# First chunk of a fused attention and expert kernel: last rows loaded in three portions, weight words asked for five blocks ahead, squares of the values behind the attention

## Chip, cores and metric

The kernel runs on one core of a Trainium2 chip. The metric is the device time of one execution in microseconds (us), as the median over runs. Engines are named as in the profile: PE (TensorE matmul, PEld its weight loads), DVE (VectorE), ACT (ScalarE), POOL (GpSimd) and SP (SyncE, which issues nearly all transfers here). PEclk is the clock granted to PE: 1.00 is 2.4 GHz, 0.50 is 1.2 GHz.

## What is computed

The reference is causal attention with a linear memory, mixed by a gate per head, then a dense squared-ReLU layer, then four experts mixed by normalised weights:

```python
scores = scale * np.matmul(q, k.transpose(0, 1, 3, 2))      # causal mask, softmax over keys
local = np.matmul(a, v)
mem_out = einsum(phi(q), M_prev) / (einsum(phi(q), z_prev) + 1e-06)
attn = g * mem_out + (1 - g) * local                          # g = sigmoid(beta)
h = np.maximum(x @ w_in, 0.0); y = (h * h) @ w_out            # x: attention, 1152 x 512; d_ff 2048
p = domain_probs / (domain_probs.sum(-1, keepdims=True) + 1e-09)
out += p[:, e:e + 1] * (np.maximum(y @ w1[e], 0.0) @ w2[e])   # four experts, d_ff 1024
```

Sizes: 2 sequences, 8 heads, 576 rows, head width 64. The dense layer's weights arrive as 64-bit words and are turned into 32-bit floats on the chip.

## The kernel before

The 1152 rows are cut into nine tiles of 128 rows (`TILES`) and three chunks of tiles (`CHUNKS`): chunk 0 is the first 128 rows of both sequences, chunk 1 is four tiles (rows 128 to 383), chunk 2 is the rest. The dense layer runs over 16 blocks of 128 hidden units, once per chunk, by `ffn1(c, ...)`. Its first run, `ffn1(0)`, is the stage this change touches; it starts near 22 us and ends near 136 us. Three streams of work run in it side by side:

- **The layer.** For each block f, `up(f)` multiplies the chunk by the up-weights (matmuls of L101, output `hpa`), ACT and DVE square the ReLU (L744, L745), and `down(f - 2)` multiplies by the down-weights (L759, outputs `y`). One step of the layer is one matmul of the program (two MATMUL records of the trace).
- **The weights.** `convert` takes 32 halves of blocks ("words", tile `w64`, 512 KB each, L682). ACT makes two pieces from a word (L694 `mag`, L697 `bits`), DVE joins them (L700, L703) and SP writes the result to DRAM (L706, `w1s`) for the two later runs. `fetch(i + 3)` asks for the word three places on. Words alternate between the tags `w0` and `w1` of pool `wp`, two buffers each, so four words have room. In this text words are counted from 0; word 9 is `w_529` in the built program before and `w_471` in the changed one.
- **The attention of chunk 1.** `attention_a` works in pairs of units over 12 pairs. `rest` sorts the parts of each pair into a list of steps: scores (L302) two pairs ahead, row maxima by `top` on DVE (L189), exponentials on ACT (L319), transposes of the probabilities on PE (L331) copied by ACT (L336), and products with the values (L351). The last steps combine memory and local parts (L213 on DVE, L214 on POOL and DVE), transpose each tile (`second`, L197, output `tp`, one PSUM buffer of tag `m`) and split it into two floats (L222 on ACT, L223 on DVE), which is what the next layer run (L106) reads.

`mix(layer, rest(...), 0.58)` takes 0.58 steps of `rest` per step of the layer, so the two are interleaved on PE in a fixed order: PE runs in program order, and what it must wait for, it waits for in place. The order on ACT, DVE, POOL and SP is chosen by the framework's scheduler when the program is built, except where `keep_in_program_order` pins an instruction; on the chip each of them runs its list in order.

Two more parts matter here. `load(r)` asks for the keys, queries and values of row block r (L271, L272, L280); `load(2)` is planned as one step at the end of pair 0. `value_scale` squares all values on ACT (L439, ten instructions: six on value tiles `va`, four on tiles `vstage` that it loads itself, L430, two buffers), adds the sums with a matmul (L443, output `total`, also PSUM tag `m`), and makes from it a power of two, `vs` (L444 and `power`), which chunk 2's attention reads later (L528). In `rest`, `value_scale` advances after steps 0 and 3 of each pair from the third on:

```python
for k, (_, f) in enumerate(sorted(at_i[i], key=lambda x: x[0])):
    f()
    if k in (0, 3) and i > 1:
        next(scale, None)
    yield
```

Of the kernel before, what the change touches and what calls it, by code (L numbers as in the profile page):

```python
# [10 lines left out]
F32 = mybir.dt.float32  # L11
# [3 lines left out]
I32 = mybir.dt.int32  # L15
# [6 lines left out]
P = 128  # L22
B, H, S, D = 2, 8, 576, 64
DM = 512
# [28 lines left out]
def attention_then_experts(ctx, tc, qa, ka, va, qc, kc, vc, mz, beta, w1, probs, w2, out):  # L53
# [11 lines left out]
    nc = tc.nc  # L65
# [7 lines left out]
    wp = ctx.enter_context(tc.tile_pool(name="wp", bufs=2))  # L73
# [39 lines left out]
    def run(g):  # L113
        for _ in g:
            pass
# [111 lines left out]
    ka_t, va_t = {}, {}  # L227
# [29 lines left out]
    def attention_a(c, pool, eng, banks):  # L257
# [6 lines left out]
            pairs += [[(t + b, kn, h, nh) for b in range(B)] for h in range(0, H, nh)]  # L264
        st, q, a_, at_, pvs, xls = {}, {}, {}, {}, {}, {}

        def load(r):
            raw = pool.tile([P, H, P], F32, tag="qa", name="qa", bufs=2)
            ka_t[r] = kva.tile([P, H, P], F32, name=f"ka{r}")
            for hs in (slice(0, 4), slice(4, 8)):  # L270
                nc.sync.dma_start(out=ka_t[r][:, hs], in_=ka[r, :, hs])  # L271
                nc.sync.dma_start(out=raw[:, hs], in_=qa[r, :, hs])  # L272
            q[r] = [raw, None, pool.tile([P, B, H, D + 1], F32, tag="xm", name="xm", bufs=2)]
            if r:
                load_v(r)

        def load_v(r):
            for b in range(B):
                va_t[b, r] = kva.tile([P, H, D], F32, name=f"va{b}_{r}")
                nc.sync.dma_start(out=va_t[b, r].rearrange("p h d -> p (h d)"), in_=va[b, r])  # L280
# [132 lines left out]
        def out_(b):  # L413
# [3 lines left out]

        return SimpleNamespace(
            pairs=pairs, load=load, load_v=load_v, phis=phis, scores=s_, turn=t_, values=v_, mem=mem, combine=combine_,
            states=states, norms=norms, recall=recall, weights=weights, local=local, out=out_,  # L420
        )
# [27 lines left out]
    def rest(x, scale):  # L449

        at_i = {}

        def plan(i, order, f):
            at_i.setdefault(i, []).append((order, f))

        plan(0, 5, lambda: x.load(2))
        for i, pair in enumerate(x.pairs):
            t, kn, h0, nh = pair[0]
            r = TILES[t][0][1] // P
            if i:  # L460
                plan(i - 2, 0, lambda p=pair: run(x.scores(p)))
            for u in pair:
                plan(i, 2, lambda u=u: x.turn(u))
            plan(i, 4, lambda p=pair: [x.values(u) for u in p])
            if h0 == 0:
                plan(i - (r > 1), 1, lambda r=r: [run(y) for y in x.phis(r)])
                for g, hs in enumerate((slice(0, 3), slice(3, 6), slice(6, 8))):
                    plan(i + g // (3 - r), 3, lambda r=r, hs=hs: x.mem(r, hs))
            if h0 + nh == H:
                for n, u in enumerate(pair):  # L470
                    parts = []

                    def make(t=u[0], parts=parts):
                        parts.extend(x.combine(t))
                        parts[0]()

                    plan(i, 5 + n, make)
                    plan(i, 7 + n, lambda parts=parts: parts[1]())
                    plan(i + 1, 1.5 + n, lambda parts=parts: parts[2]()())
        for i in sorted(at_i):  # L480
            for k, (_, f) in enumerate(sorted(at_i[i], key=lambda x: x[0])):
                f()
                if k in (0, 3) and i > 1:
                    next(scale, None)
                yield

    def attention_b(pool, ps):

# [184 lines left out]
    def convert(pool):  # L673

        todo = [x for g in range(n1 + 2) for x in ((g, 0), (g - 2, 1)) if 0 <= x[0] < n1]
        words = {}

        def fetch(i):
            if i < len(todo):
                f, half = todo[i]  # L680
                words[i] = wp.tile([P, DM, 2], I32, tag=f"w{i % 2}", name="w64")
                nc.sync.dma_start(out=words[i].rearrange("p n t -> p (n t)"), in_=w1[f, half].bitcast(I32))  # L682

        fetch(0)
        yield
        fetch(1)
        fetch(2)
        yield
        for i, (f, half) in enumerate(todo):
            fetch(i + 3)  # L690
            w64 = words.pop(i)
            mag = pool.tile([P, DM], F32, tag="mag", name="mag")

            nc.scalar.activation(out=mag, in_=w64[:, :, 1].bitcast(F32), func=AF.Abs, scale=2.0**-112)  # L694
            bits = pool.tile([P, DM], I32, tag="bits", name="bits", bufs=8)

            nc.scalar.activation(out=bits, in_=w64.bitcast(U8)[:, :, 3], func=AF.Copy, scale=2.0**-5, bias=-31.0 / 64)  # L697
            if i == 0:
                yield
            nc.vector.scalar_tensor_tensor(  # L700
                out=bits, in0=mag.bitcast(I32), scalar=3, in1=bits, op0=ALU.logical_shift_left, op1=ALU.bitwise_or
            )
            nc.vector.scalar_tensor_tensor(  # L703
                out=bits, in0=w64[:, :, 1], scalar=-(2**31), in1=bits, op0=ALU.bitwise_and, op1=ALU.bitwise_or
            )
            nc.sync.dma_start(out=w1s[f, half], in_=bits.bitcast(F32))  # L706
            made[f, half] = bits.bitcast(F32)
            yield
# [77 lines left out]
    with ExitStack() as ca:  # L786
        kva = ca.enter_context(tc.tile_pool(name="kva", bufs=1))
        aap = ca.enter_context(tc.tile_pool(name="aap", bufs=2))
        cvp = ca.enter_context(tc.tile_pool(name="cvp", bufs=2))
        cv = convert(cvp)  # L790
        mzd = kva.tile([P, H, B, D + 1], F32, name="mzd")
        with tc.tile_pool(name="ps_0", bufs=1, space=PSUM) as ps_0:
# [21 lines left out]
        with tc.tile_pool(name="ps_1", bufs=1, space=PSUM) as ps_1:  # L814
            banks[:] = ps_1, 2, 1, 1
            layer.send(ps_1)
            mix(layer, rest(c1, value_scale(aap, banks)), 0.58)
# [262 lines left out]
    for i in range(len(pairs)):  # L1080
# [5 lines left out]
        todo = iter([(j, half) for j in {0: (), 1: (4, 5), 2: (6, 7)}.get(i, (i + 5,)) for half in range(2)])  # L1086
# [80 lines left out]
```

## Time and profile before

| what | us |
|---|---|
| median of three runs (lowest, highest) | 718.51 (717.93, 721.85) |
| the profiled execution, its own time | 718.66 |
| its span, first to last instruction | 716.8 |
| around the span (718.66 - 716.8) | 1.9 |
| PE busy in the span | 676.4 (94%) |
| DVE busy | 553.3 (77%) |
| ACT busy | 428.0 (60%) |
| mean granted PE clock | 0.994 |

Busy PE time is a modelled figure of pipelined matmuls, so it shows where PE stood idle better than how close it is to its peak. Idle time of another engine costs nothing unless PE, or a transfer that PE needs, waits for it. Over the whole span DMA is busy about half the time; in the first quarter it is close to full in places.

### The profile page before, as it was taken

How to read it: one execution, taken by the hardware profiler on the slowest of the kernel's cores; microseconds unless marked ns; L12 is line 12 of the kernel's file. 1: busy time of each engine (PE TensorE's matmuls, PEld its weight loads, DVE VectorE, ACT ScalarE, POOL GpSimd, SP SyncE). 2: the span in 40 equal slices, each digit the busy share in tenths (PEclk: the TensorE clock that was granted, in tenths of full speed). 3: DMA queues.
4: the chain of work that ended last, by engine and by line, in shares of the span. 5: the costliest groups of instructions: out<-in, count | busy, mean ns of one | idle time of the engine just before them, and what ended most of it. 6: DMA issues, size and time to landing. Idle time of an engine off the chain costs nothing.

```text
span 716.8 us, 12523 instructions
## 1 busy us (share of the span) xinstructions
PE 676.4 (94%) x4604; PEld 480.9 (67%) x4604; DVE 553.3 (77%) x1107; ACT 428.0 (60%) x842; POOL 168.9 (24%) x198
## 2 busy tenths in 40 slices
PE   7788899999899998999999999999999999999997
PEld 5567677877678787999765565666655555555553
DVE  6878866499998865778798778998786776867763
ACT  5879786586565546986876648455453444444340
POOL 1001101232010032102243332544323232232300
PEclk9999999999999999999999999999999999999999
DMA  9996883378976544875313231333333131100002
GB/s 314 321 323 232 268 279 115 129 245 212 209 177 133 126 103 125 304 269 149 117 61 112 66 118 59 119 117 118 118 123 114 59 118 59 59 1 1 1 1 73
DMA packets 65421, 101.25 MB, mean 141 GB/s; under 512 B 32656, under 2 KB 34704, under 8 KB 65360
## 3 DMA queue, kind: packets, MB, share of 16 engines
q1 hardware_dynamic: 65216, 100.45, 45.5%
q8 instruction: 36, 0.59, 0.3%
q14 instruction: 25, 0.20, 0.1%
q10 hardware_dynamic: 144, 0.00, 0.0%
HBM read 82.87 MB, written 10.75 MB: 131 GB/s over the span
## 4 chain that ended last, share of the span: by engine, by line
PE 36%; DVE 8%; DMA 3%; ACT 2%; issue 2%; POOL 1%; DVEq 0%; ACTq 0%; SPq 0%; POOLq 0%
PE o L1055 19%; PE pe L963 16%; DMA raw<-in_w 3%; DVE wu L927 2%; DVE w L872 1%; DVE g L979 1%; DVE h L984 1%; ACT junk L868 1%; DVE xs L872 1%; ACT g L978 1%; ACT wu L932 0%; DVE acc L1068 0%; DVE u L984 0%; POOL u L993 0%; DVE w L84 0%
## 5 line engine op out<-in xcount | busy, mean ns | idle before, releaser
L1055 PE MATMUL o<-w,g 128*128 128x512 f16 x864 | 218.3, 379 | 7.1 <-DVE g L979 3.6
L963 PE MATMUL pe<-xs,wu 128*128 128x256 f16 (+1 forms) x1344 | 196.4, 286 | 1.6 <-DVE h L984 1.6
L963 PEld LDWEIGHTS <-wu 128*128 128x128 f16 x1344 | 130.9, 98 | 69.7 <-issue 3.4
L1055 PEld LDWEIGHTS <-g 128*128 128x128 f16 x864 | 83.8, 98 | 77.4 <-DVE g L979 6.6
L978 ACT ACTIVATE g<-h 128x512 f16<-128x512 f32 (+1 forms) x64 | 43.3, 677 | 105.7 <-DVE h L984 105.7
L761 PE MATMUL y<-g,w 128*128 128x512 f32 (+1 forms) x384 | 89.4, 369 | 0.0
L761 PEld LDWEIGHTS y<-g,w 128*128 128x128 f32 x384 | 67.7, 188 | 7.2
L979 DVE SCALAR_TENSOR_TENSOR g<-h,g 128x512 f16<-128x512 f32 (+1 forms) x64 | 50.5, 789 | 25.7 <-ACT g L978 25.5
L993 POOL TENSOR_TENSOR u<-u,p 128x256 f32<-128x256 f32 (+1 forms) x32 | 32.4, 1014 | 132.1 <-ACT p L992 111.3
L930 POOL TENSOR_TENSOR ws<-raw 128x256 f32<-128x256 f32 x32 | 23.3, 728 | 159.6 <-issue 79.7
L84 DVE TENSOR_TENSOR w<-wraw,w 128x512 fp32r<-128x512 f32 x64 | 47.8, 753 | 14.0 <-ACT w L83 13.9
L984 DVE SCALAR_TENSOR_TENSOR h<-pe,u 128x256 f32<-128x256 f32 (+1 forms) x96 | 42.9, 452 | 19.8 <-PE pe L963 15.6
L106 PE MATMUL hpb<-x,w 128*128 128x512 f32 x192 | 51.0, 401 | 4.2 <-DVE r L745 4.2
L927 DVE SCALAR_TENSOR_TENSOR wu<-ws,wpow,wu 128x512 f16<-128x512 f32 x64 | 50.0, 823 | 1.0 <-ACT wu L938 0.9
L872 DVE SCALAR_TENSOR_TENSOR w<-raw,wpow,w 128x512 f16<-128x512 f32 x64 | 48.2, 757 | 0.7 <-ACT w L871 0.6
L83 ACT ACTIVATE w<-wraw 128x512 fp32r<-128x512 f32 x64 | 39.6, 624 | 14.8 <-DMA wraw<-w1s 7.4
L868 ACT ACTIVATE junk<-raw 128x1024 bf16<-128x1024 f32 x32 | 33.6, 1050 | 20.0 <-DMA raw<-in_w 19.8
L871 ACT ACTIVATE w<-raw,wpow 128x512 f16<-128x512 f32 x64 | 44.6, 709 | 0.9 <-PE o L1055 0.9
L106 PEld LDWEIGHTS hpb<-x,w 128*128 128x128 f32 x192 | 34.9, 188 | 12.6 <-DVE r L745 5.9
L189 DVE CUSTOM_DVE_ANT_0 a<-sc,mask 128x384 f32<-128x384 f32 (+4 forms) x80 | 35.8, 479 | 7.3 <-PE sc L551 7.0
L210 POOL TENSOR_TENSOR xm<-xm,cf 128x512 f32<-128x512 f32 x7 | 8.1, 1162 | 138.0 <-DVE cf L209 94.7
L106 PE MATMUL hpc<-x,w 128*128 128x384 f32 x192 | 37.0, 338 | 1.4 <-DVE w L84 0.5
(168 smaller groups left out, 1153.2 us busy)
## 6 DMA issues: line engine op xcount, KB each, us to landing
raw<-in_w SPq DMA_DIRECT2D x64, 512.0 KB, 3.4
w<-in_w SPq DMA_DIRECT2D x32, 512.0 KB, 5.2
wraw<-w1s SPq DMA_DIRECT2D x64, 256.0 KB, 3.1
w1s<-bits SPq DMA_DIRECT2D x32, 256.0 KB, 3.3
kraw<-in_kc SPq DMA_DIRECT2D x8, 576.0 KB, 3.9
vraw<-in_vc SPq DMA_DIRECT2D x8, 320.0 KB, 4.0
qraw<-in_qc SPq DMA_DIRECT2D x4, 512.0 KB, 4.2
out<-acc SPq DMA_DIRECT2D x8, 256.0 KB, 2.1
```

What stands on the lines that cost most here:

```text
L84: eng.tensor_sub(w[:, 1], raw, w[:, 0].bitcast(F32))
L106: nc.tensor.matmul(acc, lhsT=w[:, a, kk * P:(kk + 1) * P], rhs=xs_r[c][:, b, kk, :], start=(i == 0), stop=(i == 3 * NK - 1),)
L761: nc.tensor.matmul(yacc[d], lhsT=w[:, a, d * P:(d + 1) * P], rhs=g[:, b], start=(first and i == 0), stop=(last and i == 2),)
L868: nc.scalar.activation(out=junk2, in_=raws[i, half], func=AF.Square, accum_out=wsq[:, e, half, p:p + 1])
L871: nc.scalar.activation(out=w0, in_=x, func=AF.Copy, scale=s)
L872: nc.vector.scalar_tensor_tensor(out=w1, in0=x, scalar=s, in1=w0, op0=ALU.mult, op1=ALU.subtract)
L927: nc.vector.scalar_tensor_tensor(out=w[:, 1, ks], in0=x, scalar=s1, in1=w[:, 0, ks], op0=ALU.mult, op1=ALU.subtract)
L963: nc.tensor.matmul(acc, lhsT=w[:, wa, k, kk * P:kk * P + P], rhs=x[:, xb, kk], start=(m == 0), stop=(m == 5))
L978: nc.scalar.activation(out=g[:, 0], in_=hm, func=AF.Relu)
L979: nc.vector.scalar_tensor_tensor(out=g[:, 1], in0=hm, scalar=0.0, in1=g[:, 0], op0=ALU.max, op1=ALU.subtract)
L984: nc.vector.scalar_tensor_tensor(out=out, in0=acc, scalar=HID, in1=x, op0=ALU.mult, op1=ALU.add)
L1055: nc.tensor.matmul(outs[t], lhsT=g[:, gb, r:r + P], rhs=w[:, wa], start=(p == 0 and m == 1 and k == 0), stop=(p == 3 and m == 0 and k == 2),)
```

## The change

`load` takes portions: 0 and 1 are the two halves (by heads) of keys and queries, 2 the values. `rest` plans the three portions of `load(2)` as steps of pairs 0, 1 and 2 (first half, values, second half) where one step stood at the end of pair 0; the list of steps is two longer. `value_scale` advances after every step from pair 10 on, and what is left of it runs at the end. Words go to three tags of two buffers each, the third from `convert`'s own pool, and from the second word on `fetch` is called for the words three, four and five places on, each word once.

```diff
-        def load(r):
...
+        def load(r, parts=(0, 1, 2)):
+            if 0 in parts:
+                ka_t[r] = kva.tile([P, H, P], F32, name=f"ka{r}")
...
+            for i in parts:
+                hs = slice(4 * i, 4 * i + 4)
+                if i < 2:
+                    nc.sync.dma_start(out=ka_t[r][:, hs], in_=ka[r, :, hs])
+                    nc.sync.dma_start(out=q[r][0][:, hs], in_=qa[r, :, hs])
+                elif r:
+                    load_v(r)
...
-        plan(0, 5, lambda: x.load(2))
+        for i, k, order in ((0, 0, 5), (1, 2, 5), (2, 1, 5)):
+            plan(i, order, lambda k=k: x.load(2, (k,)))
...
                 f()
-                if k in (0, 3) and i > 1:
+                if i > 9:
                     next(scale, None)
                 yield
+        yield from scale
...
-        words = {}
+        words, fetched = {}, set()
 
         def fetch(i):
-            if i < len(todo):
+            if i < len(todo) and i not in words and i not in fetched:
                 f, half = todo[i]
-                words[i] = wp.tile([P, DM, 2], I32, tag=f"w{i % 2}", name="w64")
+                fetched.add(i)
+                words[i] = (pool if i % 3 == 2 else wp).tile([P, DM, 2], I32, tag=f"w{i % 3}", name="w64")
...
-            fetch(i + 3)
+            for k in range(3 if i else 1):
+                fetch(i + 3 + k)
```

Line numbers of the changed program are some 3 to 7 higher than before from `load` on. Three places show how it moves instructions.

On SP, at the start of the layer, before: each write of a converted word (L706) is followed by one request for a word (L682), with two loads of `vstage` and three of `wraw` (weights for the next layer run) among them.

```order
L706 DMA w1s<-bits 128x512
L682 DMA w_398<-in_w 128x1024
L430 DMA vstage<-in_vc 128x4x128
L706 DMA w1s<-bits 128x512
L682 DMA w_419<-in_w 128x1024
L430 DMA vstage<-in_vc 128x4x128
L706 DMA w1s<-bits 128x512
L682 DMA w_458<-in_w 128x1024
L706 DMA w1s<-bits 128x512
L682 DMA w_467<-in_w 128x1024
L706 DMA w1s<-bits 128x512
L682 DMA w_520<-in_w 128x1024
```

The same place in the changed program (L713 is the write, L688 the request):

```order
L713 DMA w1s<-bits 128x512
L688 DMA w_398<-in_w 128x1024
L688 DMA w_400<-in_w 128x1024
L688 DMA w_402<-in_w 128x1024
L713 DMA w1s<-bits 128x512
L688 DMA w_423<-in_w 128x1024
L713 DMA w1s<-bits 128x512
L688 DMA w_462<-in_w 128x1024
L713 DMA w1s<-bits 128x512
L688 DMA w_471<-in_w 128x1024
L713 DMA w1s<-bits 128x512
L688 DMA w_524<-in_w 128x1024
```

Words 4, 5 and 6 now follow the first write, and word 9 (`w_471`) the fourth, where before word 9 (`w_529`) followed the sixth write; the three `wraw` loads have gone to a place behind some twenty more writes.

On DVE, before the row maxima (L189) of the fourth pair of chunk 1, before:

```order
L700 SCALAR_TENSOR_TENSOR bits<-mag,bits 128x512
L703 SCALAR_TENSOR_TENSOR bits<-w_520,bits 128x512
L700 SCALAR_TENSOR_TENSOR bits<-mag,bits 128x512
L189 ISA a,mx<-sc,mask 128x256
L189 ISA mx 128x1
```

And changed:

```order
L707 SCALAR_TENSOR_TENSOR bits<-mag,bits 128x512
L710 SCALAR_TENSOR_TENSOR bits<-w_462,bits 128x512
L707 SCALAR_TENSOR_TENSOR bits<-mag,bits 128x512 x2
L710 SCALAR_TENSOR_TENSOR bits<-w_471,bits 128x512
L189 ISA a,mx<-sc,mask 128x256
L189 ISA mx 128x1
```

Ahead of the maxima now stand two joins more, those of words 9 and 10.

On PE at the end of the stage, behind the last product with the values, before:

```order
L759 MATMUL y_417<-g_1343,bits 128x256 x2
L759 MATMUL y_418<-g_1343,bits 128x256 x2
L101 MATMUL hpa<-y_77,bits 128x256 x4
L759 MATMUL y_417<-g_1419,bits 128x256
L197 MATMUL tp<-ident,xl 128x128 x4
L759 MATMUL y_417<-g_1419,bits 128x256
L759 MATMUL y_418<-g_1419,bits 128x256
L197 MATMUL tp<-ident,xl 128x128 x4
```

Changed, on PE and then on ACT (L442 is the square, L222 the split of a transposed tile):

```order
L101 MATMUL hpa<-y_77,bits 128x256 x4
L766 MATMUL y_421<-g_1361,bits 128x256 x2
L766 MATMUL y_422<-g_1361,bits 128x256 x2
L197 MATMUL tp<-ident,xl 128x128 x4
L446 MATMUL total<-vsq,ones 128x10
L766 MATMUL y_421<-g_1440,bits 128x256 x2
L197 MATMUL tp<-ident,xl 128x128 x4
L766 MATMUL y_422<-g_1440,bits 128x256 x2
```

```order
L361 ACTIVATE xl<-pv 128x2x256
L442 ACTIVATE sq,vsq<-va_2_705 128x512
L442 ACTIVATE sq,vsq<-vstage 128x512 x2
L751 ACTIVATE g_1504<-hpa 128x256
L222 ACTIVATE x_75<-tp 128x4x128
L442 ACTIVATE sq,vsq<-vstage 128x512 x2
L222 ACTIVATE x_75<-tp 128x4x128
```

The matmul of `total` has moved from the middle of the stage to a place between the two transposes, directly behind the first, and the squares that it sums stand on ACT among the last copies of the stage. No instruction order differs on any engine behind this stage.

## Rows read from the trace of the kernel before

**Rows 1.** Windows: busy us (and instructions) of PE, PEld, DVE, ACT, POOL, then PEclk, DMA share, GB/s.

```profile
60.00:80.00 20.00, 18.05 (x160) 14.66 (x158) 16.24 (x34) 17.19 (x43) 3.09 (x2) 1.00 0.74 238
...
120.00:140.00 20.00, 19.45 (x136) 16.21 (x135) 7.45 (x12) 8.29 (x24) 1.49 (x1) 1.00 0.28 92
sum 120.00, PE 106.68 PEld 84.61 DVE 84.61 ACT 90.59 POOL 9.54; mean PE 17.78 PEld 14.10 DVE 14.10 ACT 15.10 POOL 1.59
```

**Rows 2.** Timeline of PE: start us, us, what, count, idle before and its releaser.

```profile
46.94 1.09 PE L331 MATMUL atp<-ident,a 128*128 128x128 f32 x4 [2.55 <-DVE mx L189]
47.82 1.92 PE L759 MATMUL y<-g,bits 128*128 128x256 f32 x4
...
50.04 1.03 PE L759 MATMUL y<-g,bits 128*128 128x256 f32 x4
...
57.07 0.66 PE L331 MATMUL atp<-ident,a 128*128 128x128 f32 x4 [1.05 <-DVE mx L189]
...
67.74 1.17 PE L351 MATMUL pv<-va,at 128*64 128x64 f32 x32 [0.76 <-ACT at L336]
```

**Rows 3.** Timeline of ACT around the wait for a word.

```profile
40.55 0.66 ACT L697 ACTIVATE bits<-w 128x512 int32<-128x512 uint8 x1
44.18 0.66 ACT L694 ACTIVATE mag<-w 128x512 f32<-128x512 f32 x1 [2.97 <-DMA w<-in_w]
```

**Rows 4.** Timeline of DVE at the same place.

```profile
45.42 0.69 DVE L700 SCALAR_TENSOR_TENSOR bits<-mag,bits 128x512 int32<-128x512 int32 x1 [2.74 <-ACT bits L697]
46.03 0.42 DVE L189 CUSTOM_DVE_ANT_0 a<-sc,mask 128x256 f32<-128x256 f32 x1
```

**Rows 5.** Timeline of SP: the first write, requests of words 7 to 9, loads of `wraw`.

```profile
22.50 0.33 SPq L706 DMA_DIRECT2D w1s<-bits  x1
...
31.03 0.38 SPq L682 DMA_DIRECT2D w<-in_w  x1
...
33.55 0.45 SPq L682 DMA_DIRECT2D w<-in_w  x1
34.05 1.42 SPq L723 DMA_DIRECT2D wraw<-w1s  x3
...
38.94 0.38 SPq L682 DMA_DIRECT2D w<-in_w  x1
```

**Rows 6.** Windows around that wait, columns as in rows 1.

```profile
42.00:44.00 2.00, 2.00 (x21) 1.51 (x20) 0.68 (x1) 0.00 (x0) 0.00 (x0) 1.00 0.80 253
...
47.00:48.00 1.00, 1.00 (x5) 1.00 (x6) 1.00 (x8) 1.00 (x4) 0.00 (x0) 0.50 1.03 412
```

**Rows 7.** Timeline of PE, later: the middle of the stage and its end.

```profile
76.80 0.55 PE L331 MATMUL atp<-ident,a 128*128 128x128 f32 x3 [1.01 <-DVE mx L189]
...
81.86 0.94 PE L364 MATMUL pm<-mzd,phia 128*128 128x130 f32 x6 [1.59 <-DVE x L223]
...
125.53 1.99 PE L759 MATMUL y<-g,bits 128*128 128x256 f32 x8
...
129.52 0.60 PE L197 MATMUL tp<-ident,xl 128*128 128x128 f32 x4
...
131.54 0.66 PE L197 MATMUL tp<-ident,xl 128*128 128x128 f32 x4 [0.55 <-DVE x L223]
```

**Rows 8.** Timeline of ACT: a square with its accumulator read, and copies of the end.

```profile
79.89 0.62 ACT L439 ACTIVATE sq<-va 128x512 bf16<-128x512 f32 x1
80.40 0.19 ACT L439 ACTIVATION_READ_ACCUMULATOR sq<-va 128x1 f32 x1
80.50 0.58 ACT L222 ACTIVATE x<-tp 128x512 fp32r<-128x512 f32 x1
...
125.65 0.60 ACT L358 ACTIVATE xl<-pv 128x512 f32<-128x512 f32 x1 [0.47 <-PE pv L351]
...
130.16 0.60 ACT L222 ACTIVATE x<-tp 128x512 fp32r<-128x512 f32 x1 [0.48 <-PE tp L197]
```

**Rows 9.** Tile `vstage`: the time from issue to landing of its four loads.

```profile
DMA to landing us min/median/max: 3.5/5.0/5.4
```

More of the change, by code (lines that the diff above doesn't have):

```diff
@@ L265, in attention_a @@
         st, q, a_, at_, pvs, xls = {}, {}, {}, {}, {}, {}
-        def load(r):
[L268 to L275, printed above, removed]
+        def load(r, parts=(0, 1, 2)):
+            if 0 in parts:
+                ka_t[r] = kva.tile([P, H, P], F32, name=f"ka{r}")
+                q[r] = [pool.tile([P, H, P], F32, tag="qa", name="qa", bufs=2), None, None]
+                q[r][2] = pool.tile([P, B, H, D + 1], F32, tag="xm", name="xm", bufs=2)
+            for i in parts:
[5 more added lines that the diff above has]
+                    load_v(r)
         def load_v(r):
```

## The prediction, made blind

> **What bounds the kernel now.** I read the windows first, to see where PE stands idle near the change. From 20 to 140 us PE is busy 106.68 of 120 us [rows 1], so 13.3 us is all that any new order in this stage can give back, apart from the clock. ACT is busy 17.19 us of the 20 between 60 and 80, and 8.29 us of the last 20 [rows 1]: the squares leave a full stretch for an emptier one.
>
> The timeline of PE then gives the single waits. The longest one in which the change has a part ends at 46.94: 2.55 us, named after DVE's maxima [rows 2]. Followed back, it is not DVE that is slow. ACT stood idle 2.97 us until 44.18 for a word [rows 3], the join of that word on DVE waited 2.74 us for ACT, and the maxima stand behind this join in DVE's list [rows 4]. The word was asked for only at 38.94, behind a gap in SP's list that words 7 and 8 (31.03, 33.55) did not have [rows 5]; it took 44.18 - 38.94 = 5.2 us. The engines of the DMA were not full meanwhile (share 0.80) [rows 6], so the request was late, not the transfer slow. The wait has a second price: behind it the granted clock is 0.50, the level of 1.2 GHz [rows 6]. Four transposes take 1.09 us and four layer matmuls 1.92 there, against 0.66 and 1.03 at 2.4 GHz [rows 2]: 0.43 + 0.89 = 1.3 us lost.
>
> **The change part by part.** The first three parts give, the last one takes.
>
> *Load in portions.* In SP's list all six loads still stand ahead of the first write, only in another order (values before second halves). I count it as nothing: what covers it is that no engine reads these tiles before the third pair. The two more steps in the list shift attention by 2 / 0.58 = 3.4 layer steps against the layer; PE's work stays.
>
> *Words five ahead.* Word 9 is now asked for behind the fourth write, where word 7 was (31.03), word 10 where word 8 was (33.55) [rows 5]. Are they there when ACT is free, at 40.55 + 0.66 = 41.2 [rows 3]? From the first write at 22.5 on, words 4 to 10 (seven times 524 KB) and five writes (262 KB each) make 5.0 MB: 12.1 us at 412 GB/s, 19.7 us at 253 [rows 6], so all of it is there between 34.6 and 42.2. ACT takes two pieces of 0.6 us from each word: word 9 until 42.4, word 10 until 43.6. DVE must now join both before the maxima, 0.61 us apiece (45.42 to 46.03 [rows 4]): start of word 10 by 44.2, rest of word 9 by 44.9. PE went 0.91 us after the maxima began (46.94 - 46.03), so now at 45.8; it gets there at 44.4 and waits 1.4 us in place of 2.55. **Gain 1.15 us**, and as no such long wait is left, **1.3 us** of clock. Bounds: 0, where the words come no sooner, and 2.55 + 1.3 = 3.9.
>
> *Less ahead of the waiting engines.* The wait of 1.05 us at 57.07 and that of 1.01 at 76.80 are again for the maxima [rows 2, 7]. In the changed list of DVE one pair of joins fewer (1.2 us) stands ahead of each: I take 0.9 and 0.7. Before the 0.76 us at 67.74 [rows 2] a square sat on ACT between the exponentials and the copies that PE waits for; a square costs 0.61 (79.89 to 80.50 [rows 8]), so 0.6 goes. At 81.86 [rows 7] a square sat ahead of the copy of `tp`; a piece of a word takes its place, but one layer step more covers it: 0.4 of 1.59. Together **2.6 us**; bounds 0 and 4.4, the four waits whole.
>
> *Squares at the end.* Let T be the end of the last product with values, 125.53. A layer step takes (129.52 - 125.53) / 9 = 0.44 us [rows 7]. Behind T now stand eight steps and the first transposes, so PE comes to the matmul of `total` at T + 3.55 + 0.5 = T + 4.0. It needs all ten squares. ACT copies the product from T + 0.1 (125.65 [rows 8], 0.5 us), then does squares 5, 6 and 7 until T + 2.45. The loads for squares 8 and 9 need the two buffers which 6 and 7 read, so SP can ask for them at T + 1.85 and T + 2.45 and not before. Such a load took 3.5, 5.0 or 5.4 us [rows 9], the long ones in the full stretch; here the DMA share is 0.28 [rows 1], so I take 3.5: T + 5.4 and T + 6.0. Square 9 ends at T + 6.6, its accumulator read 0.1 later (rows of 0.62 and 0.19, overlapped [rows 8]): T + 6.7. **PE waits 2.7 us.** Below, with loads that land at once, the copy of `tp` comes 0.64 us after the transposes begin and takes 0.6 [rows 8], T + 4.8, then two squares: T + 6.1, a wait of 2.1. Above, with 5.4: T + 8.6, a wait of 4.6. The old wait of 0.55 us at 131.54 [rows 7] goes, since two layer steps stand between `total` and the second transposes: net **2.15** (1.55 to 4.05). The nearest row for the clock behind such a wait is that of 2.55 us, behind which it fell, so I add the same **1.3** (0 to 1.3). The sum and the eight small DVE instructions for `vs` lie under two layer steps and the second transposes; even at the 0.42 us of a maximum [rows 4] each, 3.4 in all, the second copy is split by T + 11, when the stage ends. Three loads of `wraw` and two of `vstage` leave the early stretch; they have the 0.28 of the end.
>
> Sum: -1.15 - 1.3 - 2.6 + 2.15 + 1.3 = -1.6. Nothing behind the stage moves in any list, so it arrives whole: 718.66 - 1.6 = 717.06 on the profiled execution's time. The median is 0.15 below that execution (718.51), so **716.9 us**. About 0.5%, 3.6 us, is what a measurement of this kernel can tell from no change.
>
> **The rivals.**
>
> 1. *The last loads land fast.* If `vstage` lands in under 2.9 us, PE waits 2.1 to 2.3 us; say that the clock then stays at 2.4 GHz, as it does from 60 to 80 us with waits up to 1.01 in it [rows 1, 7]: 718.66 - 5.05 + 1.65 = 715.3, by the median 715.1. For it: the quiet DMA. Against: no load of this shape under 3.5 [rows 9]. The Trainium skill, in "DMA: Bandwidth & Descriptors", section on the anatomy of one DMA, fits transfers issued by GpSimd with about 2.0 us plus the bytes over 436 GB/s; for 256 KB that makes an estimate of 2.6 us, and this rival. The trace's shortest, 3.5, speaks against it, but in busier stretches.
>
> 2. *Slower: DVE's joins become the wait.* With more words on hand, joins run in front of the maxima at many pairs, as at the second place shown, where two more stand. If this takes back what the shorter lists gave (2.6) and the wait at 46.94 still costs the clock, only 1.15 is gained: 718.66 - 1.15 + 3.45 = 720.96, median 720.8. It decides if PE's waits for the maxima between 50 and 120 us stay at 2 us or more in total. For it: DVE is busy 84.61 of 120 us [rows 1] and runs its list in order. Against: the stage's joins are the same number, and words come sooner.
>
> 3. *The transfers are the bound.* If the early words share the same full engines, word 9 comes no sooner and 2.45 goes from the gain: 719.5, median 719.4. For it: at 253 GB/s the bytes end at 42.2. Against: 412 GB/s in the same stretch [rows 6].
>
> 4. *The last loads land late*, 5.4 us: 718.66 - 5.05 + 4.05 + 1.3 = 718.96, median 718.8.
>
> That a part doesn't do what it says is in the sum already: the portions change next to nothing.
>
> **How the numbers follow.** Chances: forecast 0.47, rival 1 0.22, rival 2 0.11, rival 3 0.08, rival 4 0.12. The range goes from 713.5 (rival 1 with 1.6 us more of the four waits' 4.4) to 720.9 (rival 2). It leaves out a wider gain and a stacking of rivals 2 and 4. Faster by over 0.5% means under 714.9: half of rival 1 and the forecast with most of its bounds on the good side, 0.2. Slower means over 722.1, which only rivals 2 and 4 together reach: 0.07. The rest, 0.73, is no change that can be told.
>
> **What would show it.** Right: ACT's wait for a word near 41 us gone; PE's idle before the transposes there 1.4 us or less, and clock 1.00 behind it; a wait of PE at `total` of 2 to 3 us, ended by the last square, with a lower granted clock behind. Wrong: `total` without a wait over 1 us, the early wait still there, or PE's busy share between 50 and 120 us no higher than before.

## The result and the profile after

| | before | changed |
|---|---|---|
| median of 19 runs each, us (lowest, highest) | 718.51 (716.28, 723.13) | 723.3 (719.7, 727.36) |
| ratio, 95% interval | | 1.0059 [1.0043, 1.0074] |
| the profiled execution, its own time | 718.66 | 723.08 |
| its span | 716.8 | 721.0 |
| mean granted clock | 0.994 | 0.995 |

The change is slower by 0.6%: 4.2 us by the ratio, while the medians of the table lie 4.8 us apart. The forecast was 716.9 us, and its range ended at 720.9: it was wrong, and on the wrong side. The ratios here and below leave out three executions far slower than the rest: two of the kernel before (857.86 and 857.23 us) and the profiled one of e7 (2389.8 us), for which e11 stands in.

The timeline of PE in the changed kernel, from the first wait on that the prediction speaks of (columns as in [rows 2]):

```profile
44.65 0.63 PE L334 MATMUL atp<-ident,a 128*128 128x128 f32 x4 [1.24 <-DVE mx L189]
...
54.76 0.66 PE L334 MATMUL atp<-ident,a 128*128 128x128 f32 x4 [1.50 <-DVE mx L189]
...
66.29 1.17 PE L354 MATMUL pv<-va,at 128*64 128x64 f32 x32 [0.54 <-ACT at L339]
...
75.00 0.55 PE L334 MATMUL atp<-ident,a 128*128 128x128 f32 x3 [0.66 <-DVE mx L189]
...
81.21 0.94 PE L367 MATMUL pm<-mzd,phia 128*128 128x130 f32 x6 [2.13 <-DVE x L223]
...
102.96 0.55 PE L334 MATMUL atp<-ident,a 128*128 128x128 f32 x3 [1.00 <-DVE mx L189]
```

At the first place the wait is 1.24 us in place of 2.55 [rows 2], and the four transposes behind it take 0.63, not 1.09: this part of the forecast came as written (1.4, clock 1.00). The four waits that should have shrunk by 2.6 us, 1.05, 0.76, 1.01 and 1.59 [rows 2, 7], are now 1.50, 0.54, 0.66 and 2.13: two a little shorter, two longer, and 1.00 at 102.96 is a further one. From 50 to 120 us PE is busy 62.95 us of 70, and 64.50 before (62.83 and 64.00 in a second profile of each, e6 and e5 below): a sign of being wrong that the prediction had named, while its signs of being right all came too.

The end of the stage, again on PE, with `y` of L766 as the layer:

```profile
125.73 0.92 PE L354 MATMUL pv<-va,at 128*64 128x64 f32 x24
...
130.13 0.60 PE L197 MATMUL tp<-ident,xl 128*128 128x128 f32 x4
133.18 0.39 PE L446 MATMUL total<-vsq,ones 128*128 128x10 f32 x2 [2.45 <-ACT sq L442]
133.43 2.04 PE L766 MATMUL y<-g,bits 128*128 128x256 f32 x4
135.26 1.06 PE L197 MATMUL tp<-ident,xl 128*128 128x128 f32 x4
136.11 3.13 PE L766 MATMUL y<-g,bits 128*128 128x256 f32 x12
138.89 8.56 PE L106 MATMUL hpb<-x,w 128*128 128x512 f32 x36
```

The wait at `total` is 2.45 us (predicted: 2 to 3, likeliest 2.7). Behind it four layer matmuls took 2.04 us (1.03 before) and the transposes 1.06 (0.60). The windows show the clock there (columns as in [rows 1]):

```profile
82.00:84.00 2.00, 2.00 (x14) 1.24 (x14) 0.00 (x0) 0.84 (x2) 0.00 (x0) 0.56 0.95 339
...
133.00:137.00 4.00, 3.82 (x13) 3.22 (x14) 1.09 (x10) 0.73 (x3) 0.00 (x0) 0.57 0.00 0
```

The granted clock was 0.57 behind the wait of 2.45, and 0.56 behind that of 2.13 at 81.21, near the level of 1.2 GHz. On ACT, the last two squares stand behind the copy of `tp`, and the first of them waits 0.22 us for its load:

```profile
130.77 0.60 ACT L222 ACTIVATE x<-tp 128x512 fp32r<-128x512 f32 x1 [1.38 <-PE tp L197]
131.59 0.63 ACT L442 ACTIVATE sq<-vstage 128x512 bf16<-128x512 f32 x1 [0.22 <-DMA vstage<-in_vc]
...
132.41 0.63 ACT L442 ACTIVATE sq<-vstage 128x512 bf16<-128x512 f32 x1
```

DVE was done with its part of that copy 1.0 us before the last square ended (131.40 + 0.69 = 132.09, and 132.41 + 0.63 = 133.04):

```profile
131.40 0.69 DVE L223 TENSOR_TENSOR x<-tp,x 128x512 fp32r<-128x512 f32 x1 [0.87 <-ACT x L222]
```

SP asked for the loads at 128.54 and just behind:

```profile
128.54 0.99 SPq L433 DMA_DIRECT2D vstage<-in_vc  x2
```

In tile `vstage`, asked for this stretch alone, the two landed after:

```profile
DMA to landing us min/median/max: 3.0/3.1/3.2
```

### The profile page after: what moved, and what is told of

It reads as the page before. It is cut to its first block, busy times and chain, and to the rows that moved or that the text cites. A ratio compares the mean times of both kernels' runs of the same rounds, so it can differ in the third digit from the quotient of the medians.

```text
span 721.0 us, 12530 instructions
## 1 busy us (share of the span) xinstructions
PE 679.0 (94%) x4604; PEld 482.8 (67%) x4604; DVE 552.7 (77%) x1107; ACT 428.9 (59%) x842; POOL 168.4 (23%) x198
## 4 chain that ended last, share of the span: by engine, by line
PE 56%; DVE 20%; ACT 11%; DMA 6%; issue 5%; POOL 1%; DVEq 0%; SPq 0%; ACTq 0%; POOLq 0%
PE o L1062 20%; PE pe L970 18%; PE y L768 4%; DMA raw<-in_w 4%; PE hpc L106 3%; PE hpb L106 3%; PE y L766 2%; DVE w L84 2%; PE pv L624 2%; DVE a L189 2%; ACT a L322 2%; ACT junk L875 2%; DVE g L986 1%; PE hpa L101 1%; DVE bits L707 1%
## 5 line engine op out<-in xcount | busy, mean ns | idle before, releaser
L84 DVE TENSOR_TENSOR w<-wraw,w 128x512 fp32r<-128x512 f32 x64 | 46.3, 730 | 12.2 <-ACT w L83 12.1
L189 DVE CUSTOM_DVE_ANT_0 a<-sc,mask 128x384 f32<-128x384 f32 (+4 forms) x80 | 35.9, 479 | 9.0 <-PE sc L556 7.0
L210 POOL TENSOR_TENSOR xm<-xm,cf 128x512 f32<-128x512 f32 x7 | 7.7, 1106 | 137.2 <-DVE cf L209 92.2
```

Of the source, the lines that this page charges most:

```text
L84: eng.tensor_sub(w[:, 1], raw, w[:, 0].bitcast(F32))
L189: nc.vector.tensor_tensor_reduce(out=dst, in0=sc, in1=msk, op0=ALU.add, op1=ALU.max, scale=1.0, scalar=-3.0e38, accum_out=m)
```

## The experiments

Twelve runs (nine new kernels, and three that profile a kernel once more), each against the kernel before on the same chip (its medians there: 717.85 for e1 to e4, 718.54 for e5 to e8, 718.36 for e9 to e11 and 718.01 us for e12). Three theories were on the table for the 0.6%: the price lies in the stage's end (tail theory); it lies in the middle, from the order of the words (A), from the two steps more (B), or from the squares that left (C).

**One part at a time.** e1 takes only the words five ahead, e2 only the squares, e3 only the load in portions:

```diff
 e1
-            fetch(i + 3)
+            for k in range(3 if i else 1):
+                fetch(i + 3 + k)
 e2
-                if k in (0, 3) and i > 1:
+                if i > 9:
                     next(scale, None)
...
+        yield from scale
 e3
-        plan(0, 5, lambda: x.load(2))
+        for i, k, order in ((0, 0, 5), (1, 2, 5), (2, 1, 5)):
+            plan(i, order, lambda k=k: x.load(2, (k,)))
```

> Before, with words asked for five blocks ahead and nothing else. Seen in the changed kernel: the early wait for a word shrank (2.6 us gained), the waits of PE between 50 us and the last product with values grew from 5.5 to 7.0 us with 1.6 us of lower clock behind one of them (3.2 us lost), and the matmul of the sum at the end cost about 3.8 us. Theory A: the loss in the middle comes from joins and word pieces that stand ahead of maxima and of copies of the transposed tiles, so from the words: this run gives 718.5 - 2.6 + 3.2 = 719.1. Theory B: it comes from the shift by two steps that the portions bring: 715.9 here. Theory C: it comes from the squares leaving the middle, so that other work of ACT moves up: 715.9 here. In all three PE's wait before the transposes near 45 us is 1.2 to 1.5 us in place of 2.55 and PE has no wait at the sum.

> Before, with the squares behind the attention and nothing else. Tail theory: PE waits 2 to 3 us at the matmul of the sum, with a lower clock behind it, about 3.8 us in all. Theories A and B of the middle: 718.5 + 3.8 = 722.3, less up to 1.3 us for the two waits with a square ahead. Theory C: 718.5 + 3.8 + 3.2 = 725.5. The early wait of 2.55 us stays (word 9 is still asked for late).

> Before, with the last rows in three portions (and so two steps more in the list) and nothing else. Theories A and C: nothing to tell from before, 718.5 (within 1 us), with the waits of the middle at about 5.5 us. Theory B: 718.5 + 3.2 = 721.7, with waits of the middle near 7 us.

Measured: e1 718.67 us, ratio 1.0003 [0.9983, 1.0023]; e2 721.58, 1.0061 [1.0036, 1.0087]; e3 718.38, 1.0015 [1.0000, 1.0031]. The squares alone cost what the whole change costs; words and portions alone cost nothing that can be told. B falls. The words, from which the forecast drew 2.45 of its 5.05 us of gain, give none that can be told. By its number alone e1 fits theory A (719.1 / 718.5 = 1.0008); e7 below decides that. On PE in e2 the wait at `total` is there in the same size, although neither the words nor the load differ from before; here the profile names DVE's copy of `tp` as what ended it, and not the last square:

```profile
131.37 0.36 PE L443 MATMUL total<-vsq,ones 128*128 128x10 f32 x2 [2.50 <-DVE x L223]
```

**The sum moved.** e4 is the changed kernel with `total` three steps later, behind the layer:

```diff
             yield
+        yield
+        yield
+        yield
         total = banks[0].tile([P, vsq.shape[1]], F32, tag="m", name="total", bufs=banks[2])
```

> The changed kernel, with three empty steps ahead of the matmul of the sum, so that it comes behind the layer's last matmul. Tail theory: the wait of 2.45 us and the lower clock behind it (1.9 us) go, the old wait of about 0.5 us at the second transposes comes back: 723.3 - 3.8 = 719.5. Rival: the wait only moves, because the squares are late wherever the sum stands and the next layer run then waits for the second copy or the sum: 722.5 to 723.5.

Measured: 719.25 us, 1.0017 [0.9999, 1.0035]. With the wait gone, 0.42 of the 0.59% goes, and the old wait at the second transposes is back. On PE:

```profile
130.71 0.66 PE L197 MATMUL tp<-ident,xl 128*128 128x128 f32 x4 [0.55 <-DVE x L223]
...
132.94 0.39 PE L449 MATMUL total<-vsq,ones 128*128 128x10 f32 x2
```

**Where is the gain of the words?** In e2 and e3 the words were asked for three ahead, as before, and yet PE's first wait was 1.01 and 0.33 us. So the 2.55 of [rows 2] may belong to that one execution. e5 and e6 profile the kernel before and the changed one once more, without an edit.

> The kernel before, profiled once more. Theory D: the long wait for the late word, from which the forecast took 2.45 us, belongs to the one execution shown. Then ACT waits 1 to 1.5 us for the word asked for near 38.5 us (not 2.97), PE waits at most 1.2 us at the transposes near 45 us (not 2.55), the granted clock behind them is 1.00, and what PE waits at the maxima near 55 us is nearer to 1.9 than to 1.05. Rival (the forecast's reading): the request is late whenever the kernel runs; ACT waits over 2.5 us, PE over 2 us, and the clock falls behind it. Time 718 us by both.

> The changed kernel, profiled once more. What belongs to the kernel comes again, what belongs to one execution does not. Tail theory: PE waits 2.3 to 2.7 us at the matmul of total again, and the first transposes of the late product to the stage's end take 8 to 9 us (6.2 in the kernel before). Theory A: PE waits 1.3 to 1.6 us near 54.8 and about 2.1 us at the product with the memory near 81 again. Theory D: the lower clock behind these two waits does not come at the same places. Time 723 us by all.

Single times 714.92 and 720.7 us. In e5, on PE and then on ACT:

```profile
46.13 0.63 PE L331 MATMUL atp<-ident,a 128*128 128x128 f32 x4 [0.33 <-DVE mx L189]
...
55.69 0.66 PE L331 MATMUL atp<-ident,a 128*128 128x128 f32 x4 [1.81 <-DVE mx L189]
```

```profile
42.90 0.69 ACT L694 ACTIVATE mag<-w 128x512 f32<-128x512 f32 x1 [0.87 <-DMA w<-in_w]
```

ACT waited 0.87 us for the word in place of 2.97 [rows 3], PE 0.33 in place of 2.55, and the next wait was 1.81 in place of 1.05. The word had been asked for as late as before (39.04, and 38.94 in [rows 5]); it landed after 3.8 us in place of 5.2. In e6, on PE:

```profile
81.30 1.64 PE L367 MATMUL pm<-mzd,phia 128*128 128x130 f32 x6 [2.14 <-DVE x L223]
...
133.35 0.39 PE L446 MATMUL total<-vsq,ones 128*128 128x10 f32 x2 [2.42 <-ACT sq L442]
133.59 1.11 PE L766 MATMUL y<-g,bits 128*128 128x256 f32 x4
134.54 0.60 PE L197 MATMUL tp<-ident,xl 128*128 128x128 f32 x4
134.97 2.75 PE L766 MATMUL y<-g,bits 128*128 128x256 f32 x12
```

The waits of the changed kernel at 81 and at `total` come again to within 0.03 us; the lower clock comes again at 81 (six matmuls take 1.64, not 0.94) and not behind `total` (1.11, not 2.04), so that from the first transposes to the stage's end it took 7.1 us and not the 8 to 9 expected. In e5, too, the waits of 0.76, 1.01, 1.59, 0.39 and 0.55 us of the kernel before came again to the hundredth, and that of 1.05, the next one behind the late word, did not (1.81). In these executions the waits that an order makes are the kernel's; the late landing and the places of the lower clock are one execution's.

**Two combinations.** e7 is the change without its third part (`if k in (0, 3) and i > 1` as before). e8 is e2 with the three empty steps of e4.

> The change without its third part: words five ahead and the load in portions, squares as before. If the parts add up, it is 1.0003 times 1.0015: ratio 1.002, 719.2 us, and no wait over 0.6 us at the matmul of total. Theory A in its strong form (the middle of the stage loses about 3 us when words and portions come together): ratio 1.004 or more, 721 us. Forecast's reading of the words: ratio 0.997.

> The kernel before with the squares behind the attention, and three empty steps ahead of total, so that this matmul comes behind the layer. Tail theory: the whole price of the third part was PE's wait at total, so ratio 1.000 to 1.002 (718 to 719.3 us), without a wait at total. Rival (Theory C: the squares gone from the middle change the order there for the worse): ratio 1.004 or more. Forecast's reading of the squares that leave the middle (0.6 and 0.4 us gained): ratio 0.9985, 716.8 us.

Measured: e7 718.43 us, 0.9993 [0.9971, 1.0014]; e8 719.78, 1.0015 [0.9991, 1.0039]. Without the squares' move the change costs nothing, so A and its strong form fall; with `total` out of the way, moving the squares costs nothing that can be told, so C falls. In e8's trace the wait at the second transposes is 1.56 us in place of 0.55, since there a square that waits for its load stands on ACT ahead of the copy of `tp`; a cost of this 1.0 us lies inside the interval.

**Squares sooner.** e9 is e4 with `if i > 7` in place of `if i > 9`.

> The changed kernel, but the squares begin two pairs sooner, and three empty steps stand ahead of total, so that this matmul comes right behind the last product with values. Tail theory: with all ten squares done by then, neither total nor the copies of tp wait for a square, the stage ends as in the kernel before, and the ratio is 0.998 to 1.001. If the squares cost as much wherever they stand (they only move their wait, here to the copies of the last two pairs), the ratio stays at 1.004 or more, with waits of PE of 2 us or more in all at the products with values from 110 to 127 us.

Measured: 722.57 us, 1.0047 [1.0024, 1.0071]: a miss for the tail theory as put there. `total` did not wait, but the squares now sit on ACT ahead of the copies of the probabilities:

```profile
114.34 0.57 PE L354 MATMUL pv<-va,at 128*64 128x64 f32 x12 [1.08 <-ACT at L339]
...
121.24 0.57 PE L354 MATMUL pv<-va,at 128*64 128x64 f32 x12 [0.81 <-ACT at L339]
```

These are rows of PE. The two waits, 1.89 us together, are new; no wait of 0.3 us or more stands there in the changed kernel. That is close to the 2 us of the other expectation, whose ratio it has. The profile of e9 also shows the lower clock near 8 us and near 84, for which it gives no reason.

**What makes the wait at `total`?** In e10 squares 8 and 9 read tiles that are long there, in place of the last two loads (the scale of the values so comes out of other numbers). e11 is e7 again, for its profile.

```diff
-            if i in (3, 4, 7, 8):
+            if i in (3, 4):
                 parts.append(stage(*todo[len(parts) - 6]))
+            if i in (7, 8):
+                parts.append(parts[i - 7])
```

> The changed kernel, but squares 8 and 9 read the first chunk's first two tiles of values again, in place of the last two loads of vstage, so the scale of the values comes out of other numbers. If the landing of the loads makes the wait at total (the forecast's step), PE waits at most 1 us there and the ratio falls to 1.002. If ACT's list makes it (squares 8 and 9 stand behind the copy of tp, which waits for the transposes), PE still waits 1.9 to 2.2 us in place of 2.45, and the ratio stays at 1.004 to 1.006.

> Words five ahead and the load in portions, squares as before, for its profile. Tail theory: no wait at total over 0.6 us, and from the first transposes of the late product to the stage's end 4.5 to 5 us. Theory A: waits of about 1.5 us near 55, 2 us near 81 and 1 us near 102 as in the changed kernel. Time 718 to 719 us.

e10: 720.47 us, 1.0029 [1.0008, 1.0050], between both expectations, and so is the wait on PE:

```profile
131.06 0.39 PE L448 MATMUL total<-vsq,ones 128*128 128x10 f32 x2 [1.41 <-DVE x L223]
```

Without the late loads 1.0 us of it is gone. Not all of that need be the landing: in the changed kernel squares 8 and 9 stand behind the copy of `tp` on ACT, and in e10 the scheduler put them ahead of it, so the loads and this place in the list have gone together. But neither expectation explains the rest: on ACT the last square ran well ahead of that,

```profile
128.82 0.62 ACT L444 ACTIVATE sq<-va 128x512 bf16<-128x512 f32 x1
129.34 0.19 ACT L444 ACTIVATION_READ_ACCUMULATOR sq<-va 128x1 f32 x1
129.69 0.60 ACT L222 ACTIVATE x<-tp 128x512 fp32r<-128x512 f32 x1 [0.16 <-PE tp L197]
```

and DVE read `tp` from 130.32 on:

```profile
130.32 0.69 DVE L223 TENSOR_TENSOR x<-tp,x 128x512 fp32r<-128x512 f32 x1 [0.86 <-ACT x L222]
```

The squares were done at 129.5 and PE went when this row ended. `total` has the PSUM tag `m`, as `tp` has, and behind the start of the layer that tag has one buffer (`banks[:] = ps_1, 2, 1, 1`, the third is its count). e11 took 719.13 us, showed no wait at `total` and the waits of 1.45 near 55 and 1.66 near 81; the 1 us near 102 was absent.

e12 puts `total` into a buffer of another tag, on top of e10:

```diff
-tag="m", name="total", bufs=banks[2])
+tag="s", name="total", bufs=banks[1])
```

> The kernel without the two late loads (squares 8 and 9 read the first two tiles of values again), and total takes a PSUM buffer of the tag s, of which there are two, in place of the one buffer of the tag m that tp holds. Buffer theory: the 1.41 us that PE still waited at total without the late loads were for the copies of tp out of that one buffer, since the last square was done 1.5 us sooner. Then the wait at total is under 0.3 us, the second transposes wait 0.4 to 0.6 us as in the kernel before, and the ratio is 1.000 to 1.002. Rival (PE waits for the squares or for DVE's list): the wait at total stays over 1 us and the ratio at 1.003.

Measured: 718.84 us, 1.0011 [0.9988, 1.0034]. On PE:

```profile
128.37 0.60 PE L197 MATMUL tp<-ident,xl 128*128 128x128 f32 x4
128.90 0.39 PE L448 MATMUL total<-vsq,ones 128*128 128x10 f32 x2
129.15 1.11 PE L768 MATMUL y<-g,bits 128*128 128x256 f32 x4
130.62 0.63 PE L197 MATMUL tp<-ident,xl 128*128 128x128 f32 x4 [0.36 <-DVE vs L130]
```

The wait at `total` is gone: its causes are the shared buffer and the late last squares (late by their loads and by their place on ACT, which no run separates). From the changed kernel over e10 to e12 it goes 2.45, 1.41, 0 us and the ratio 1.0059, 1.0029, 1.0011. The intervals of e10 and e12 overlap; it is the wait that tells them apart. No version was faster than the kernel before by more than the noise; e7, at 0.9993, is the lowest. The buffer alone, with the late loads left in, was not tried; an estimate from the rows of the changed kernel is that it gives little, as the copy was done there 1.0 us before the last square.

## Why the prediction was wrong

Two steps failed, the gains that were booked: 2.45 us for the words and 2.6 us for the shorter lists, 5.05 in all. e4, the change without the wait at `total`, measures them together: +1.2 us (-0.1 to +2.5). Between -1.6 as forecast and +4.2 as measured lie 5.8 us, and these 5.05 are most of them.

**Words five ahead (gain 1.15 + 1.3): a step that failed.** The wait after the change is in the trace with the size that was worked out (1.24 against 1.4). What failed is the base: the working took the wait of 2.55 us and the clock behind it from one execution as the kernel's own. Its reading of the 2.97 us, a late request and no slow transfer, was wrong in its second half. In all five profiles with words three ahead word 9 was asked for 5.4 to 6.7 us behind word 8, so the late request was the kernel's; but the word landed after 5.2 and 3.8 us (the kernel before), 3.6, 3.9 and 5.3 (e2, e3, e8). Of the 2.1 us between the two waits of ACT in the kernel before, 1.4 are this landing. In the five executions profiled with words three ahead PE's wait there was 2.55 and 0.33 (the kernel before), 1.01, 0.33 and 1.39 (e2, e3, e8), 1.12 on average; in the eight with words five ahead 1.24 and 1.22 (the changed kernel), 0.95, 0.54, 1.21, 0.58, 1.23 and 0.94 (e1, e4, e9 to e12), 0.99. That is a gain of 0.1 us. The granted clock from 44 to 52 us was under 1.00 in the first of these thirteen and in no other, so the 1.3 us were no gain. e1 agrees: 1.0003, from -1.2 to +1.7 us by its interval.

**Less ahead of the waiting engines (gain 2.6): the other step that failed, wrong in sign in the trace.** The waits of PE of 0.3 us or more, without the first, add up to 4.8 us until 120 in the profile on which the forecast rests, to 5.6 in e5, and to 7.0 and 7.1 in the two of the changed kernel. Of the maxima near 57 the step said that one pair of joins fewer stands ahead. The trace does not bear this out: three joins stand there as in the kernel before (at 53.11, 54.52 and 55.86), two of them twice as long as the 0.61 counted. DVE's timeline of the changed kernel:

```profile
50.47 1.38 DVE L707 SCALAR_TENSOR_TENSOR bits<-mag,bits 128x512 int32<-128x512 int32 x1 [0.24 <-ACT bits L704]
51.88 1.42 DVE L710 SCALAR_TENSOR_TENSOR bits<-w,bits 128x512 int32<-128x512 int32 x1
53.22 0.41 DVE L752 SCALAR_TENSOR_TENSOR g<-hpa,g 128x256 f32<-128x256 f32 x1
53.55 0.68 DVE L707 SCALAR_TENSOR_TENSOR bits<-mag,bits 128x512 int32<-128x512 int32 x1
54.15 0.55 DVE L189 CUSTOM_DVE_ANT_0 a<-sc,mask 128x384 f32<-128x384 f32 x1
```

From 49.32 to the maxima DVE has no gap over 0.24 us in this list. By this row PE's time saved at the first place came back here as a longer wait, as it did in e5, where the first wait was 0.33 and this one 1.81. It is not so in every profile: in e1 the two are 0.95 and 0.76, in e12 0.94 and 0.84. At 81 the copy of `tp` stands on DVE (80.47) behind other joins, and the layer step more did not cover it. The 0.6 and 0.4 us for the squares that left can be read in e2, which moves nothing else: 0.76 stayed at 0.74, and 1.59 became 1.33 with a new wait of 0.57 us at 78.86. How much of the 1.4 to 2.3 us by which the waits grew reaches the time stays open: e7, which has the words and the portions too, is at 0.9993, and e11's sum is 6.0.

**Squares at the end (2.15 + 1.3): right in size, incomplete in cause.** PE reached `total` at 133.18 - 2.45 = 130.73, 4.1 us behind the end of the last product (126.6), predicted 4.0; the last square was done 6.5 behind it, predicted 6.7. The loads landed in 3.0 to 3.2 us, not 3.5. The wait was 2.45, 2.42 and 2.50 in three executions, predicted 2.7. What the step missed is that `total` needs the buffer of `tp`. In the changed kernel this is hidden, since the last square ended behind the copy. Its lower bound of 2.1 us, for loads that land at once, kept the last squares behind that copy; with the loads gone the scheduler moved them ahead, and the wait was 1.41, all of it for the buffer (e10), and 0 with a buffer of another tag (e12). Of the clock: it was lower behind this wait in one of the three executions, there for 1.0 + 0.5 + 0.4 = 1.9 us (2.04 - 1.03, 1.06 - 0.60, 3.13 - 2.75 of e6), predicted 1.3 each time.

**The portions (nothing):** e3, 1.0015 with an interval that touches 1, does not speak against it.

**The sum by these terms:** words -0.1, tail 2.45 - 0.55 = 1.9, and 3.8 where the clock falls: +1.8 to +3.7 us, against the 4.2 measured (3.1 to 5.3 by the interval). The tail measured by itself, the changed kernel against e4, is 0.42% or 3.0 us. That is a difference between two ratios, each with an interval of its own, of 0.15 to 0.18% either way. What is left, 0.1 to 0.2% in e4, e8 and e12, is not told apart from nothing.

**The rivals.** Rival 1 (loads under 2.9 us) missed its condition by little, 3.0 measured; that the clock stays up behind such a wait did come in e6 and e2, and would have been worth 1.9 us. The 2.6 us that the prediction worked out from the Trainium skill ("DMA: Bandwidth & Descriptors", section on the anatomy of one DMA) are an estimate; the measured 3.0 decides. Rival 2 had the right sign and nearly its time (720.8), but for another reason: the waits for the maxima were over 2 us before the change already (1.05 + 1.01 [rows 2, 7]), so its test could not tell the two cases apart, and e1 shows that the joins cost nothing that can be measured. Rival 3 had priced the words' gain that did not come (719.4), but its reason failed: word 9 came sooner, and ACT took it at 40.02 without a wait (44.18 before). Rival 4 (late loads) did not come. The range was too narrow above because no rival took both gains away whole (rival 2 left 1.15 us of them): without that of the words the forecast's own terms, -2.6 + 3.45, give 719.4 by the median, still inside it, and without both 722.0, 1.3 us from the result.

## What to carry to other kernels

A wait that rests on one late landing has to be seen in a second execution before its removal is booked as gain, while the waits that the order made here came back within hundredths. When an instruction moves, list all that it needs at the new place, its PSUM buffer among them and not its inputs alone: here a tile in the one buffer of a transpose waited 1.41 us for the copies out of it. Time that PE gains ahead of an engine with a list without gaps can come back as a wait at that engine's next result.

## What was not expected of the hardware

- The two joins of 1.38 and 1.42 us at 50.47 and 51.88 ran while POOL worked at the products of L210; the next, 0.68 us, ran behind them. The same is in the kernel before, at 53.11 and 54.52.

```profile
50.26 2.49 POOL L210 TENSOR_TENSOR xm<-xm,cf 128x512 f32<-128x512 f32 x2 [46.03 <-DVE cf L209]
```

- The granted clock did not follow from a wait of the same length at the same place. Each of the thirteen profiles has a wait of 2.12 to 2.16 us near 35 us, for `phia`; from 36 to 40 us the clock was 0.57 to 0.68 in seven of them and 1.00 in six. Behind the 2.13 or 2.14 us near 81 it fell in the changed kernel (twice) and in e9, and stayed at 1.00 in e4, e10 and e12. A term for the clock is thus at best a share of the executions.
